# The border between attention gradient and last stage: turning the last dS block on TensorE, and the loads in the order of the program

## The chip, the cores and the metric

The kernel runs on one core of a Trainium2 chip. The core has a matrix engine (TensorE, PE in the profile; its weight loads are PEld), a vector engine (VectorE, DVE), a scalar engine (ScalarE, ACT), a general one (GpSimd, POOL) and a queue that only issues transfers (SyncE, SP). Sixteen DMA engines move data. Each engine runs its own instructions in order and waits for others by semaphores. The metric is the device time of one execution in microseconds; the time before is the median of three executions.

## The reference

One transformer block with adaptive layer norm, its output and the gradients of all its inputs but one bias. There are 2048 tokens of width 512, 32 heads of width 16, and a dense part of width 1792 with a squared ReLU:

```python
h = _layernorm(x) * (1 + ca) + sa
x = x + ga * A(h, wqkv, wo)            # attention
h = _layernorm(x) * (1 + cb) + sb
x = x + gb * B(h, w1, b1, w2, b2)      # dense part
out, vjp = jax.vjp(f, A_x, A_wqkv, A_wo, B_w1, B_b1, B_w2, B_b2, c, w_mod)
grads = vjp(grad_out)
```

All arrays are bf16. What matters here is the end of the backward pass: the gradients dQ, dK and dV of attention, and from them the gradient of the block's input, of `wqkv`, and of the modulation weights.

## The kernel before, in words

The attention gradient goes over eight groups of four heads (`hg`), four chunks of 512 keys (`kc`), four chunks of 512 queries (`qc`) and four tiles of 128 queries in each (`qi`). One (hg, kc, qc, qi) is a unit, four units are a block; there are 512 units and 128 blocks. For a unit, PE makes the scores of four heads (`score`), ACT their exponentials E (`expo`), PE the products dO V (`dp_pair`, two heads at a time into a tile of two PSUM banks), and DVE multiplies both into dS (line 1616). dS is used twice. As it stands it goes into the gradient of K (`k_quad`), while E goes into that of V (`v_quad`); both add into one bank, `accVK`. Turned over it goes into the gradient of Q (`dq_quad`), which sums over a whole block into a bank `dqacc`. `dq_out` scales this sum on ACT into `dqtmp`, and POOL adds it to the sum over key chunks (line 1708).

The turning has two ways. Most units go through a DMA transpose that SP issues (`transpose_unit`): two units at once (1 MB, line 1633) or one (line 1631). The fourth unit of every odd block is turned by PE against an identity matrix (`pe_turn`, eight 128x128 transposes into one bank) and copied to SBUF by ACT (line 1774). For the very last block, number 127, the third unit is turned on PE as well (`last_turn`), and DVE copies the fourth. The units one and two of block 127 still go through a DMA transpose.

The order of the instructions on each engine is written out by hand, in two strings of tokens (`order_t` for a block after an odd one, `order_n` otherwise): s is a score, e an exponential, D a dP pair, q a K or V quad, t and T a turn and its copy, d and Q the dQ matmuls and their output, f a filler matmul that adds nothing. After the last block two passes follow in which only the late tokens still do something.

The last stage (pool `phJbig` and below) has dK, dV and dQ as rows of 128 features by 2048 tokens in twelve tiles `xs["vk", 0..7]` and `xs["dq", 0..3]`. Four of these and half of another are still loaded from DRAM (lines 1792 and 1793); the other 64 rows of `xs["dq", 3]`, which come from the last group of heads, are copied within SBUF by four DMAs that POOL issues (line 1799). The weights `wT_all` (1.5 MB) are loaded at line 1797. Then:

- All twelve tiles are turned on PE into token rows (`dq_tok`, `dvk_tok`), two groups of eight 128x128 transposes for a tile (line 1941), 24 groups in all; DVE copies two out of three groups, ACT the third.
- A row loop over 16 tiles of 128 tokens: `dh1` multiplies the twelve tiles with the weights into `pdh` (line 1881), DVE and ACT do the gradient of the layer norm, `row_sums` adds up two rows on PE, `dx_out` stores the input's gradient. `load_x` fetches the input and an earlier gradient for two tiles at a time, into three buffers.
- Twelve products `dwqkv` for the gradient of `wqkv` (line 1914): four with `dq_tok`, four with the first half of `dvk_tok`, four with its second half. Between them stands the work on the modulation weights.

In this stage PE, ACT and DVE follow the program's order; SP's loads and stores are placed by the framework's scheduler. A tile in SBUF takes the place of tiles of the stage before, and its first writer waits until those are no longer used.

Of the kernel before, what the change touches and what calls it, by code (L numbers as in the profile page):

```python
# [14 lines left out]
AF = mybir.ActivationFunctionType  # L15
# [5 lines left out]
P = 128  # L21
# [13 lines left out]
def kernel(  # L35
# [1512 lines left out]
    with ExitStack() as ph:  # L1548
# [53 lines left out]
        def dp_pair(u, pair):  # L1602
# [14 lines left out]
            if qi == 3 and on_pe(u // 4):  # L1617
                held["dS"] = dS_u
            if u == NU - 2:
                held["last"] = dS_u  # L1620
# [4 lines left out]
        def transpose_unit(u):  # L1625
            hg, kc, qc, qi = units[u]
            if qi == 0:
                dqt[u // 4] = tpool.tile([P, 4, 16, P], BF, name="dsT", tag="dsT")
            if on_pe(u // 4) and qi >= 2:
                if qi == 2 and u < NU - 2:  # L1630
                    SP.dma_start(out=dqt[u // 4][:, qi], in_=bst[u][1].rearrange("p h k -> p (h k)"), transpose=True)
# [18 lines left out]
        def last_turn(half):  # L1650
            pt = psx.tile([P, 8, P], BF, name="ptL", tag=("ps0", "ps1")[half])
            for i in range(8):
                kt = i % 4
                PE.transpose(pt[:, i, :], held["last"][:, 2 * half + i // 4, kt * P:(kt + 1) * P], identb[:])
            ACT.activation(dqt[NU // 4 - 1][:, 2, 8 * half:8 * half + 8, :], pt[:], AF.Identity)
# [26 lines left out]
        def dq_quad(b, kt):  # L1682
            hg, kc, qc, _ = units[4 * b]
            if kt == 0:
                cur["dq"] = psx.tile([P, 512], F32, name="dqacc", tag="px")
# [7 lines left out]
        def dq_out(b):  # L1693
# [5 lines left out]
            if kc == 0:  # L1699
# [29 lines left out]
        with tc.manual_schedule(engines={PE.engine, ACT.engine, DVE.engine, SP.engine, POOL.engine}):  # L1729
# [4 lines left out]
            for b in range(NU // 4 + 3):  # L1734
                toks, bank = order_t if on_pe(b - 1) else order_n
                for tok in toks:
# [26 lines left out]
                    elif c == "f" and 0 < nq < 2 * NU:  # L1763
                        keep_warm()
                    elif c == "t" and 0 <= b - 1 < NU // 4:
                        if b == NU // 4:
                            last_turn(i - 1)
                        pe_turn(b - 1, i - 1)
                    elif c == "T" and 0 <= b - 1 < NU // 4:
                        dst, pt = held.pop(i - 1)  # L1770
                        if b == NU // 4:
                            DVE.tensor_copy(dst, pt[:])
                        else:
                            ACT.activation(dst, pt[:], AF.Identity)  # L1774
# [8 lines left out]
    with ExitStack() as ph:  # L1783
        big = ph.enter_context(tc.tile_pool(name="phJbig", bufs=1))
# [3 lines left out]
        psw = ph.enter_context(tc.tile_pool(name="psJw", bufs=3, space=bass.MemoryType.PSUM))  # L1788
        xs["dq", 1], xs["dq", 2], xs["vk", 4], xs["vk", 5] = (hsets[1][key] for key in ("q", "k", "v", "do"))
# [4 lines left out]
        sums = big.tile([P, 6, D], F32, name="sums_bc")  # L1794
        dmod = big.tile([P, 6, D], BF, name="dmod_bc")
        wT = big.tile([P, 12, D], BF, name="wT_all")
        SP.dma_start(out=wT[:], in_=wT_st.rearrange("j p d -> p j d"))
        for h in range(4):
            POOL.dma_start(out=xs["dq", 3][64 + DH * h:64 + DH * h + DH, :], in_=dq_last[32 * h:32 * h + DH, :])
# [4 lines left out]
        def load_x(g):  # L1804
            x0s[g] = big.tile([P, 2, D], BF, name="x0J", tag="x0J", bufs=3)
            SP.dma_start(out=x0s[g][:], in_=x_dram[:, 2 * g:2 * g + 2, :])
            dx1s[g] = big.tile([P, 2, D], BF, name="dx1J", tag="dx1J", bufs=3)
            SP.dma_start(out=dx1s[g][:], in_=dx1_st[:, 2 * g:2 * g + 2, :])

        load_x(0)  # L1810
        load_x(1)
        wms, wtags = {}, ["wmodJ0", "wmodJ1", "wmodJ2"]

        def wmod_tile():
            wtags.append(wtags.pop(0))
            return big.tile([P, 3 * D], BF, name="wmodJ", tag=wtags[-1], bufs=1)

        wmod_tile()
        wmod_tile()
        dvk_tok = [big.tile([P, 4, TT, P], BF, name=f"dvk_tok{i}") for i in range(2)]  # L1820
        wmod_tile()
# [28 lines left out]
        def c_grad(k, h):  # L1850
            part = slice(3 * D * h, 3 * D * h + 3 * D)
            prod = wk.tile([P, 3 * D], BF, name="cprod", tag="cprod", bufs=1)
# [19 lines left out]
        def norm_tile(t):  # L1872
            xns[t] = wk.tile([P, D], BF, name="xn1b", tag="xn1b", bufs=3)
# [4 lines left out]
        def dh1(t):  # L1878
# [8 lines left out]
            prod1 = wk.tile([P, D], BF, name="prod1", tag="prod1", bufs=3)  # L1887
# [23 lines left out]
        def dwqkv(b, ic):  # L1911
# [4 lines left out]
            if b == 0:  # L1916
                wblk = wk.tile([P, D], BF, name="wqblk", tag="prod1", bufs=3)
                ACT.activation(wblk[:], pw[:], AF.Identity)
                SP.dma_start(out=rows[:, 0:D], in_=wblk[:])
            else:  # L1920
                for i in range(2):
                    srcv = pw.rearrange("p (g v d) -> p g v d", v=2, d=DH)[:, :, 1 - i, :]
                    wblk = wk.tile([P, D], BF, name="wqblk", tag=("prod1", "dxn1")[i], bufs=3)
# [126 lines left out]
```

## Time and profile before

| | |
|---|---|
| median of three executions | 2481.53 us (2478.23, 2481.53, 2486.11) |
| the profiled execution | 2484.38 us |
| its span in the profile | 2482.6 us |
| mean granted PE clock | 0.984 |
| attention gradient ends, last score product (dP) of PE starts | 2365.23 us |
| first row product (`pdh`) starts | 2388.73 us |
| last weight-gradient output issued | 2479.29 us |

Times within the profile count from the start of the span. A line of the timeline gives start and length in microseconds, engine, source line, operation, output and inputs, count, and in brackets how long the engine stood idle before and what ended that. PE lines overlap, since matmuls are pipelined. SPq is SP's queue: its length is the time for which the queue was held by issuing, not that of the transfer.

### The profile page before, as it was taken

How to read it: one execution, taken by the hardware profiler on the slowest of the kernel's cores; microseconds unless marked ns; L12 is line 12 of the kernel's file. 1: busy time of each engine (PE TensorE's matmuls, PEld its weight loads, DVE VectorE, ACT ScalarE, POOL GpSimd, SP SyncE). 2: the span in 40 equal slices, each digit the busy share in tenths (PEclk: the TensorE clock that was granted, in tenths of full speed). 3: DMA queues.
4: the chain of work that ended last, by engine and by line, in shares of the span. 5: the costliest groups of instructions: out<-in, count | busy, mean ns of one | idle time of the engine just before them, and what ended most of it. 6: DMA issues, size and time to landing. Idle time of an engine off the chain costs nothing.

```text
span 2482.6 us, 49937 instructions
## 1 busy us (share of the span) xinstructions
PE 2319.5 (93%) x18967; PEld 782.2 (32%) x19052; DVE 1838.7 (74%) x2379; ACT 2302.5 (93%) x3560; POOL 491.3 (20%) x665
## 2 busy tenths in 40 slices
PE   8899899989998998899999999999999999999999
PEld 3232233223322332442333223332233322333244
DVE  6555354355445554578999999999999999999976
ACT  7999999999999999639999999999999999999954
POOL 3111222332544352101111101101011010110100
PEclk9999999999998999999999999999999999999999
DMA  4467463267647775979999999999999999999994
GB/s 148 128 171 177 143 145 102 80 175 131 90 94 160 151 134 104 246 226 169 205 200 206 199 198 205 201 202 206 203 209 197 210 205 202 200 201 220 200 268 134
DMA packets 1187551, 437.17 MB, mean 176 GB/s; under 512 B 1063915, under 2 KB 1158569, under 8 KB 1186926
## 3 DMA queue, kind: packets, MB, share of 16 engines
q1 hardware_dynamic: 1150334, 388.56, 79.2%
q0 software_dynamic: 20000, 27.35, 6.8%
q10 hardware_dynamic: 16976, 18.07, 2.7%
q8 instruction: 149, 2.44, 0.4%
q14 instruction: 92, 0.75, 0.1%
HBM read 98.30 MB, written 70.80 MB: 68 GB/s over the span
## 4 chain that ended last, share of the span: by engine, by line
ACT 40%; PE 38%; issue 8%; DVE 7%; DMA 4%; ACTq 1%; POOL 0%; SPq 0%; DVEq 0%; another core or an unknown queue 0%; POOLq 0%
ACT E_u L1600 24%; ACT ET L578 12%; PE dqacc L1690 4%; PE psST L576 3%; PE psS_A L1594 3%; DMA dsT<-dS_u 2%; ACT dsT L1774 2%; PE accVK L1663 2%; PE pm L233 2%; PE oacc L592 2%; PE psS_B L1594 2%; PE pdh L1881 2%; PE pm L424 2%; PE pm L500 2%; PE pm L410 2%
## 5 line engine op out<-in xcount | busy, mean ns | idle before, releaser
L1616 DVE TENSOR_TENSOR dS_u<-psD_u,E_u 128x1024 bf16<-128x1024 f32 x1024 | 1185.4, 1218 | 66.5 <-PE psD_u L1614 24.2
L578 ACT ACTIVATE ET<-psST 128x1024 bf16<-128x1024 f32 x1024 | 942.4, 1242 | 16.2 <-PE psST L576 15.7
L1600 ACT ACTIVATE E_u<-psS_A 128x512 bf16<-128x512 f32 x768 | 508.9, 663 | 9.6 <-DMA out_dram<-xlast 7.2
L1600 ACT ACTIVATE E_u<-psS_B 128x512 bf16<-128x512 f32 x768 | 502.1, 654 | 7.6 <-issue 1.9
L1614 PE MATMUL psD_u<-iv,ido 32*128 32x512 bf16 x2048 | 408.8, 387 | 0.4 <-DVE dS_u L1616 0.2
L576 PE MATMUL psST<-qt_sb,kt_sb 32*128 32x512 bf16 x2048 | 315.5, 388 | 45.6 <-ACT ET L578 39.2
L1600 ACT ACTIVATE E_u<-psS_C 128x512 bf16<-128x512 f32 x512 | 333.6, 652 | 2.5 <-PE psS_B L1594 0.9
L1594 PE MATMUL psS_B<-ik,iq 32*128 32x512 bf16 x768 | 294.4, 383 | 9.8 <-ACT E_u L1600 2.4
L1594 PE MATMUL psS_A<-ik,iq 32*128 32x512 bf16 x768 | 293.0, 382 | 11.3 <-DVE dwlast L237 1.0
L1708 POOL TENSOR_TENSOR dQacc<-dQacc,dqtmp 128x512 f32<-128x512 f32 x64 | 81.2, 1269 | 849.0 <-ACT dqtmp L1703 849.0
L1594 PEld LDWEIGHTS <-iq 32*128 32x128 bf16 x2048 | 130.1, 91 | 313.4 <-issue 296.2
L1663 PE MATMUL accVK<-dS_u,qz 128*32 128x512 bf16 x2048 | 213.1, 388 | 0.4 <-DVE dS_u L1616 0.2
L592 PE MATMUL oacc<-ET,vaug 128*32 128x512 bf16 x2048 | 208.5, 397 | 3.9 <-DVE ostage L596 3.9
L1672 PE MATMUL accVK<-E_u,dOs_tok 128*16 128x512 bf16 x2048 | 203.1, 385 | 0.0
L1594 PE MATMUL psS_C<-ik,iq 32*128 32x512 bf16 x512 | 193.7, 378 | 4.3
L576 PEld LDWEIGHTS <-kt_sb 32*128 32x128 bf16 x2048 | 84.9, 91 | 326.5 <-issue 305.5
L1690 PE MATMUL dqacc<-dsT,KS_tok 128*32 128x512 bf16 x2048 | 146.4, 384 | 17.0 <-DMA dsT<-dS_u 3.3
L251 DVE COPY part<-pm 128x512 f32<-128x512 f32 (+2 forms) x106 | 65.2, 615 | 120.4 <-PE pm L233 110.9
L1774 ACT ACTIVATE dsT<-ptT 128x1024 bf16<-128x1024 bf16 x126 | 142.8, 1134 | 6.7 <-PE ptT L1646 6.3
L1614 PEld LDWEIGHTS <-ido 32*128 32x128 bf16 x2048 | 105.4, 91 | 101.2 <-issue 94.8
L1663 PEld LDWEIGHTS <-qz 128*32 128x32 bf16 x2048 | 58.5, 94 | 177.2 <-issue 162.2
L1708 POOL TENSOR_TENSOR dQst<-dQacc,dqtmp 128x512 bf16<-128x512 f32 x32 | 40.6, 1268 | 264.1 <-ACT dqtmp L1703 264.1
(420 smaller groups left out, 2687.3 us busy)
## 6 DMA issues: line engine op xcount, KB each, us to landing
p_st<-part POOLq DMA_DIRECT2D x36, 256.0 KB, 4.6
kt_sb<-qkT_st POOLq DMA_DIRECT2D x124, 64.0 KB, 2.9
wA<-in_B_w_dram SPq DMA_DIRECT2D x28, 256.0 KB
wB<-w1T_st SPq DMA_DIRECT2D x21, 256.0 KB
wA<-w2T_st SPq DMA_DIRECT2D x21, 256.0 KB
wB<-in_B_w_dram SPq DMA_DIRECT2D x21, 256.0 KB
p_st<-part POOLq DMA_DIRECT2D x28, 192.0 KB, 5.2
p_st<-part SPq DMA_DIRECT2D x18, 256.0 KB
```

What stands on the lines that cost most here:

```text
L576: PE.matmul(ps[:, hi, :], kt_sb[r:r + 32, kt * P:(kt + 1) * P], qt_sb[r:r + 32, :], start=True, stop=True, tile_position=(r, 0))
L578: ACT.activation(ET[:, 2 * pair:2 * pair + 2, :], ps[:], AF.Exp, scale=SCALE)
L592: PE.matmul(oacc[32 * hq:32 * hq + 32, :], lhsT, ET[:, hq, :], start=(kt == 0), stop=(kt == TT - 1), tile_position=(0, 32 * hq), skip_grou ...
L1594: PE.matmul(psS[:], st["q"][r:r + 32, qt * P:(qt + 1) * P], st["k"][r:r + 32, kc * 512:kc * 512 + 512], start=True, stop=True, tile_positi ...
L1600: ACT.activation(bst[u][0][:, hq, :], sst.pop((u, hq))[:], AF.Exp, scale=SCALE)
L1614: PE.matmul(psD[:, hi, :], st["do"][r:r + 32, qt * P:(qt + 1) * P], st["v"][r:r + 32, kc * 512:kc * 512 + 512], start=True, stop=True, til ...
L1616: DVE.tensor_tensor(dS_u[:, 2 * pair:2 * pair + 2, :], psD[:], E_u[:, 2 * pair:2 * pair + 2, :], ALU.mult)
L1663: PE.matmul(cur["vk"][32 * hq:32 * hq + 32, :], hst[hg]["qz"][:, qt, hq, :], bst[u][1][:, hq, :], start=(qt == 0), stop=False, tile_positi ...
L1672: PE.matmul(acc[32 * hq:32 * hq + DH, :], dOs_tok[:, qt, (hg * 4 + hq) * DH:(hg * 4 + hq + 1) * DH], E_u[:, hq, :], start=False, stop=(qt ...
L1690: PE.matmul(acc[32 * hq:32 * hq + 32, :], KS_tok[:, kc * 4 + kt, h * DH:h * DH + 32], tT[:, :, hq * 4 + kt, :], start=(kt == 0), stop=(kt ...
L1708: POOL.tensor_tensor(dst2, dst, tmp[:], ALU.add)
L1774: ACT.activation(dst, pt[:], AF.Identity)
```

## The change

It has five parts, all of them at the border between the two stages.

- All four units of block 127 are turned on PE. `last_turn(j)` is now called for j from 0 to 7 (unit j // 2, half j % 2): 0 to 3 at the first t token, 4 to 7 at the second. The targets are the three single banks (`ps0`, `ps1`, `px`; the first again for j = 7) and two tiles of two banks each from the pool of the dP products (j = 3 and 4 in one, 5 and 6 in the other): seven banks. ACT copies j = 0, 1, 4, 7, DVE the others. The DMA transpose of block 127 goes.
- The last dQ block sums in bank `ps1`, and DVE scales it and adds it to the sum over key chunks in one operation straight from PSUM (line 1712 after), in place of ACT and POOL.
- The tiles of the last stage stand in two pools. `phJlow` takes those that are loaded or used in the row loop, `phJbig` the weights and the token rows. So the two sets lie over other tiles of the stage before: the weights' load waits for the last E quad and the last dS, the first load of the input waits for the last dQ matmuls and the last turn copies.
- SP follows the program's order in the last stage too. The four copies of 64 rows are issued by SP, after the first `load_x`; `load_x` in the loop stands at the end of its turn instead of at its start.
- The second half of `dvk_tok` (four tiles) is turned by four DMA transposes, issued in turns 3, 5, 7 and 9 of the row loop, in place of eight of the 24 groups on PE.

```diff
+            if u >= NU - 4:
+                held[qi] = dS_u
+            elif qi == 3 and on_pe(u // 4):
                 held["dS"] = dS_u
-            if u == NU - 2:
-                held["last"] = dS_u
...
+            if u >= NU - 4:
+                return
             if on_pe(u // 4) and qi >= 2:
-                if qi == 2 and u < NU - 2:
+                if qi == 2:
                     SP.dma_start(out=dqt[u // 4][:, qi], in_=bst[u][1].rearrange("p h k -> p (h k)"), transpose=True)
...
-        def last_turn(half):
-            pt = psx.tile([P, 8, P], BF, name="ptL", tag=("ps0", "ps1")[half])
+        def last_turn(j):
+            qi, half = j // 2, j % 2
+            if j in (3, 5):
+                held["pd"] = psd.tile([P, 2, 8, P], BF, name="ptL2", tag="pd")
+            if 3 <= j < 7:
+                pt = held["pd"][:, (j - 3) % 2]
+            else:
+                pt = psx.tile([P, 8, P], BF, name="ptL", tag=("ps0", "ps1", "px")[j % 7])[:]
             for i in range(8):
                 kt = i % 4
-                PE.transpose(pt[:, i, :], held["last"][:, 2 * half + i // 4, kt * P:(kt + 1) * P], identb[:])
-            ACT.activation(dqt[NU // 4 - 1][:, 2, 8 * half:8 * half + 8, :], pt[:], AF.Identity)
+                PE.transpose(pt[:, i, :], held[qi][:, 2 * half + i // 4, kt * P:(kt + 1) * P], identb[:])
+            dst = dqt[NU // 4 - 1][:, qi, 8 * half:8 * half + 8, :]
+            if j in (0, 1, 4, 7):
+                ACT.activation(dst, pt, AF.Identity)
+            else:
+                DVE.tensor_copy(dst, pt)
...
-                cur["dq"] = psx.tile([P, 512], F32, name="dqacc", tag="px")
+                cur["dq"] = psx.tile([P, 512], F32, name="dqacc", tag="ps1" if b == NU // 4 - 1 else "px")
...
-            if kc == 0:
+            if b == NU // 4 - 1:
+                DVE.scalar_tensor_tensor(out=st["dq"][:, qc * 512:(qc + 1) * 512], in0=acc[:], scalar=SCALE, in1=dst,
+                                         op0=ALU.mult, op1=ALU.add)
+            elif kc == 0:
...
+                    elif c == "t" and b == NU // 4:
+                        for j in range(4 * i - 4, 4 * i):
+                            last_turn(j)
...
+        low = ph.enter_context(tc.tile_pool(name="phJlow", bufs=1))
         big = ph.enter_context(tc.tile_pool(name="phJbig", bufs=1))
...
+        ph.enter_context(tc.manual_schedule(engines={PE.engine, ACT.engine, DVE.engine, SP.engine}))
...
+        load_x(0)
         for h in range(4):
-            POOL.dma_start(out=xs["dq", 3][64 + DH * h:64 + DH * h + DH, :], in_=dq_last[32 * h:32 * h + DH, :])
+            SP.dma_start(out=xs["dq", 3][64 + DH * h:64 + DH * h + DH, :], in_=dq_last[32 * h:32 * h + DH, :])
...
-        with tc.manual_schedule(engines={PE.engine, ACT.engine, DVE.engine}):
-            for k, (key, i) in enumerate(order):
+        if True:
+            for k, (key, i) in enumerate(o for o in order if o[0] == "dq" or o[1] < 4):
...
-                if t % 2 == 0 and t >= 2 and t // 2 + 2 < TT // 2:
-                    load_x(t // 2 + 2)
...
+                if t in (3, 5, 7, 9):
+                    i = 4 + (t - 3) // 2
+                    SP.dma_start(out=dvk_tok[1][:, i - 4], in_=xs["vk", i][:], transpose=True)
...
+                if t % 2 == 0 and t >= 2 and t // 2 + 2 < TT // 2:
+                    load_x(t // 2 + 2)
```

Left out are the lines in which `sums`, `dmod`, the `wmod` tiles, `cprod`, `xn1b`, `prod1` and the tiles of `load_x` change their pool, and where tiles are named earlier or later in the program without other effect.

## The prediction

> **What bounds the kernel now.** I read the page first (the span, the engines' shares), then the chain of waits over the last 120 us, then the timeline around the border between the attention gradient and the last stage, then SP's own queue, then the half-microsecond windows there. The page shows a kernel in which PE and ACT are each 93% busy; such a kernel has few gaps, and a change at one border can only be worth what stands still there.
>
> ```profile
> span 2482.6 us, 49937 instructions
> PE 2319.5 (93%) x18967; PEld 782.2 (32%) x19052; DVE 1838.7 (74%) x2379; ACT 2302.5 (93%) x3560; POOL 491.3 (20%) x665
> ```
>
> The chain of waits at the border (start, length, what): the reader is to see two transfers, 8.22 and 12.50 us, between the last score work and the first row product (pdh), with 16 dQ matmuls between them.
>
> ```profile
> 2365.62 0.38 PE ptL L1654 x5
> 2366.00 8.22 DMA dsT<-dS_u
> 2374.27 1.86 PE dqacc L1690 x16
> 2376.18 12.50 DMA wT_all<-wT_st
> 2388.73 0.39 PE pdh L1881
> ```
>
> SP's queue (start, time the queue was held): a transpose of 1 MB holds it for about 5 us, so the last one, though its data was ready, is issued at 2366.00, and every load of the last stage waits behind it.
>
> ```profile
> 2360.93 4.97 SPq L1633 DMA_TRANSPOSE dsT<-dS_u  x1
> 2366.00 4.87 SPq L1633 DMA_TRANSPOSE dsT<-dS_u  x1
> 2370.93 0.58 SPq L1792 DMA_DIRECT2D iq<-dQc  x1
> 2373.53 0.51 SPq L1793 DMA_DIRECT2D qz<-dQc  x1
> 2376.18 0.38 SPq L1797 DMA_DIRECT2D wT_all<-wT_st  x1
> ```
>
> The timeline, with idle time before each and its releaser, shows that PE is nearly as late as the weights: after its 3.31 us of waiting it has turns until 2388.3 and then waits only 0.38 us. So both have to become shorter.
>
> ```profile
> 2374.27 1.84 PE L1690 MATMUL dqacc<-dsT,KS_tok 128*32 128x512 bf16 x16 [3.31 <-DMA dsT<-dS_u]
> 2378.45 2.07 POOL L1799 DMA_DIRECT2D qz<-dQst  x4 [0.30 <-POOL dQst L1708]
> 2387.29 0.61 PE L1941 MATMUL ptq<-identb,qz 128*128 128x128 bf16 x8 [1.05 <-DVE dvk_tok L1947]
> 2388.73 0.39 PE L1881 MATMUL pdh<-wT_all,iq 128*128 128x512 bf16 x1 [0.38 <-DMA wT_all<-wT_st]
> DMA to landing us min/median/max: 7.0/7.1/7.3
> ```
>
> The last of these lines belongs to the four copies of line 1799: 2380.0 + 7.1 is 2387.1, just before 2387.29. The DVE copy named there ended at 2385.8, so the 1.05 us were a wait for those copies. The windows (PE, PEld, DVE, ACT, POOL busy; granted clock; DMA share; GB/s) show the clock at half after the idle stretch and two transfer rates.
>
> ```profile
> 2373.50:2374.00 0.50, 0.00 (x0) 0.00 (x0) 0.00 (x0) 0.00 (x0) 0.00 (x0) 1.00 1.02 369
> 2375.00:2375.50 0.50, 0.50 (x12) 0.17 (x4) 0.00 (x0) 0.00 (x0) 0.00 (x0) 0.50 1.37 377
> 2380.00:2380.50 0.50, 0.50 (x13) 0.50 (x11) 0.45 (x2) 0.47 (x1) 0.50 (x2) 1.00 1.06 156
> 2383.00:2383.50 0.50, 0.50 (x13) 0.50 (x10) 0.45 (x2) 0.50 (x1) 0.00 (x0) 1.00 1.10 352
> 2385.00:2385.50 0.50, 0.50 (x13) 0.50 (x11) 0.50 (x2) 0.18 (x2) 0.00 (x0) 1.00 0.95 158
> ```
>
> **The change, part by part.** Nothing before the last block changes, so times to 2365.55 stand. From there I set the new order against the old rows.
>
> *Turns of the last block.* Four groups of eight PE transposes become eight (0.49 us from group to group, 2365.55 to 2366.04); one DMA transpose goes. Groups 0 to 3 run to 2367.4, the E quad and two filler matmuls to 2368.1. Group 4 shares a two-bank tile with group 3 and waits for DVE's copy of it: last dS ends 2367.1, two copies at 0.69 (row L1772; 0.61 back to back) end 2368.4. Group 6 waits likewise for the copy of group 5: 2370.3. Group 7 ends 2371.2. ACT's four copies at 1.02 (row L1655) end 2372.5 and hold up nobody. Fillers and the last two quads take 0.86 (2368.33 to 2369.19 before), to 2372.05; two dQ blocks at 0.95 each then end at 2373.9 instead of 2376.1. Gain here 2.2; the 3.3 us wait and the half clock behind it (1.7 us lost: 3.4 us at half) go.
>
> *Last dQ by VectorE.* ACT 0.60 and POOL 1.27 are replaced by one DVE operation. No row has its shape: 0.42 (L1904, bf16 difference) and 1.22 (L1616, twice the elements from PSUM) bound it; L1906, the same operation, took 0.75, and I take 0.7. It delays DVE's first turn copy by that much, which the four banks there hide; without them it would cost 0.7.
>
> *Fewer turns in the last stage.* 24 groups become 16: PE loses 8 x 0.445 = 3.6, DVE five copies, ACT three. From 2373.95, the first 14 groups end at 2380.2. In their place SP issues four transposes of 512 KB inside the row loop, about 2.2 us of queue each (row L1631: 2.02 to 2.31) while the DMA share is 0.66, then 0.21 (2400 to 2440); they are wanted at about 2464. I cost them at nothing; the cover is that slack, and its loss is a rival below.
>
> *Weights.* Their tile now lies where the E and dS buffers were, so the load waits for the last E quad, 2372.05, not for dQ and the last copies: issue 2372.4 instead of 2376.18. The four big loads ahead of it issue at 2366.0 instead of 2370.93.
>
> *The four row copies* (the 64 rows of the last dQ) move from POOL's queue to SP's, behind weights, x0 and dx1. This is where the gain is spent. Data of the last transpose stopped at 2372.9 and landed 2374.27: 1.4 us. In order, before: 2.1 MB at 376 GB/s to 2378.6; the 64-row load and POOL's copies, narrow, some 0.5 MB at 160 to 180, and 1.57 MB of weights at 352 (4.45 us) give about 2387.1, landed 2388.5; measured 2388.73, so the order holds. After: data from 2368.1; four loads to 2373.8; 64 rows (1.8) to 2375.6; weights to 2380.1, landed 2381.5; x0 and dx1 (0.52 MB, 1.5) to 2381.6; four copies (issued by 2378.2) 1.3 to 2.4, landed 2384.7. The 7.1 us of before, from 2378.2, would say 2385.3. Bounds: all at 376 GB/s, 2382.0; the weights' own 12.5 us again, then 1.5 and 2.4, 2388.8. I take 2384.7, next to both middle values.
>
> The Trainium skill ("DMA: Bandwidth & Descriptors", Queues, rings and completion order) says that each DMA engine takes a queue's descriptors in ring order. By that rule a copy put behind the weights can't pass them; the landing worked out above agrees.
>
> PE then stands from 2380.2 to 2384.7, and needs two more groups, 0.9, before pdh. Clock: 3.3 us of idling was followed by 3.4 us at 0.50, and 1.05 us (2386.2) by none; 4.5 lies beyond the first, so I take the same 1.7 us (bounds 0 and 3.4, twice as long at half).
>
> The Trainium skill ("TensorE: Matmul & The Clock Gate", Part 1) says that a wholly idle free-running window of some 3.4 us throttles. By that rule 4.5 us of idling need not contain one; then the sum would be 1.7 us better.
>
> **Sum.** Pdh starts in effect at 2384.7 + 0.9 + 1.7 = 2387.3, 1.4 us earlier than 2388.73. The row loop (PE 19.95 of 20 us) and the weight products after it keep their length. The profiled execution took 2484.38 around its span of 2482.6, 2.85 over the median of 2481.53; less 1.4 it is 2483.0, or 2480.1 at the median. I say 2480.
>
> **Rivals.**
> *Copies in time.* If the narrow copies do not wait for x0 and dx1, or the DMA runs at its best rate, PE is the bound: 2373.95 + 16 x 0.445 + 0.15 = 2381.2, 7.5 us gained, 2474.0. For it: 16 groups are all that PE has; against it: 352 GB/s on the weights and the order found above.
> *The row loop starves (slower).* SP in program order puts each x0 load behind an output store that waits for DVE's dx, and behind a transpose. Load of pair 3 issues about 11.7 us after pdh starts and is wanted at 20.3. It decides when landing takes over 8.6 us: were it 12.5 as for the weights, 3.9 are lost at first and about 1.4 at each of four later pairs, 9.5 in all: 2480.1 + 9.5 = 2489.6. Against it: the DMA share there.
> *Copies at the late end.* Landed 2388.8, pdh in effect at 2391.4: 2.7 lost, 2484.2. The change then does not do what it says: one wait takes the place of another.
>
> **How the numbers follow.** Forecast 0.55, copies in time 0.24, late end 0.12, starving 0.09. About 0.3% (7.4 us) is what a measurement of this kernel can tell: faster means below 2474.1, which holds the greater part of "in time", 0.17; slower is starving, 0.09; the rest, 0.74, is no change that can be told. The range 2473.0 to 2485.5 takes in the bounds of the copies and leaves out starving and a little of "in time". The forecast's own: 2477 to 2482.5.
>
> **What would show it.** The last dQ matmuls end near 2373.9 with no DMA named ahead of them; the weights issue near 2372.4 and land by 2382; PE's longest wait in the border stands before the transposes of qz, 3 to 5 us, released by a DMA of the row copies, with the clock at half after it. Wrong if that wait is missing, if pdh waits for the weights instead, or if PE has gaps in the row loop ended by DMA or ACT.

## The result: slower by 0.35%, and the profile after

Nineteen executions of the changed kernel have a median of 2488.34 us (2482.91 to 2499.88), nineteen of the kernel before, run beside them, 2480.71 us (2475.03 to 2489.85). The ratio is 1.0035, with a 95% interval of 1.0023 to 1.0047. The forecast was 2480.0 us in a range of 2473.0 to 2485.5, so it was wrong. Nearest came the rival of the starving row loop, priced at 2489.6 with a chance of 0.09. A second series of the two kernels, run 6 below, has a smaller difference (ratio 1.0014).

The profiled execution of the changed kernel took 2487.6 us. Its page shows nothing of the loss, since 8 us are 0.3% of the span:

```profile
span 2485.8 us, 49959 instructions
PE 2323.8 (93%) x19020; PEld 781.9 (31%) x19020; DVE 1835.2 (74%) x2377; ACT 2300.6 (93%) x3558; POOL 487.0 (20%) x660
```

In this trace the border went as forecast. In the timeline after (start, length, engine, line, what; in brackets the idle time before and its releaser) SP has the four big loads under way at 2364.38 in place of 2370.93, the weights at 2371.53 in place of 2376.18, and then the four row copies. Below stand the last dS, by which I line up the kernels (it ends at 2364.51 + 1.21 = 2365.72, and at 2367.12 before, so 1.40 us of each difference in time stem from what lies ahead), PE's wait for the copies and the first row product.

```profile
2364.38 0.57 SPq L1807 DMA_DIRECT2D iq<-dQc  x1
2364.51 1.21 DVE L1616 TENSOR_TENSOR dS_u<-psD_u,E_u 128x1024 bf16<-128x1024 f32 x1
...
2371.53 0.88 SPq L1813 DMA_DIRECT2D wT_all<-wT_st  x1
...
2374.42 2.47 SPq L1826 DMA_DIRECT2D qz<-dQst  x4
...
2383.36 1.63 PEld L1953 LDWEIGHTS <-qz 128*128 128x128 bf16 x16 [4.48 <-DMA qz<-dQst]
...
2385.05 0.63 PE L1893 MATMUL pdh<-wT_all,iq 128*128 128x512 bf16 x1
```

The windows after (PE, PEld, DVE, ACT, POOL busy; granted clock; DMA share; GB/s) show what that wait costs: the clock is at 0.50 behind it, and the share of the DMA engines is 1.09 while PE stands.

```profile
2379.72:2381.72 2.00, 0.00 (x0) 0.00 (x0) 0.00 (x0) 0.39 (x1) 0.00 (x0) 1.00 1.09 223
2381.72:2383.72 2.00, 0.33 (x4) 0.36 (x5) 0.00 (x0) 0.00 (x0) 0.00 (x0) 0.88 1.09 288
2383.72:2385.72 2.00, 2.00 (x17) 1.63 (x15) 1.12 (x2) 0.00 (x0) 0.00 (x0) 0.50 1.05 391
```

Then the row loop, from the first `pdh` to the first weight product (`pwq`), takes 53.32 us in place of 47.92. The chain of waits says why. Before, it ran through PE's row products (shares by line, from 2389 to 2436 us):

```profile
by line: PE pdh L1881 87.2%; PE rsumJ L1900 13.2%; issue 0.6%
```

After, it alternates between a store that has to land, a transpose that holds SP's queue, and at the end a load of the input:

```profile
2397.13 2.27 DMA out_dram<-dx1J
2399.42 0.33 SPq L1822
...
2399.80 3.02 SPq L1973
...
2402.87 0.57 SPq L1838
...
2403.55 3.80 DMA out_dram<-dx1J
...
2407.80 3.07 SPq L1973
...
2411.60 3.92 DMA out_dram<-dx1J
...
2416.39 3.56 SPq L1973
...
2420.67 4.72 DMA out_dram<-dx1J
...
2430.54 5.77 DMA x0J<-in_A_x_dram
...
2436.39 0.82 ACT xn1b L1886
```

From one store to the next SP needs 2411.60 - 2403.55 = 8.05 us: the store lands (3.86 to the issue of the `dx1` load, which takes over the stored buffer), that load's issue (0.34), the transpose (3.07), the modulation weights (0.57), and gaps. PE needs 6.04 us for the same two tiles. So the input's loads are issued 6.4, 8.0, 9.1 and 9.4 us after one another (2397.62, 2404.04, 2412.08, 2421.16, 2430.54), and the loop falls behind them. ACT's waits in the loop (total, times, longest) and the place where PE at last stands:

```profile
ACT xn1b L1886 <- DMA x0J<-in_A_x_dram: 13.6, 3, 7.3
...
PE rsumJ L1912 <- DVE s12a L1900: 4.0, 1, 4.0
```

PE hides most of ACT's first two waits (1.24 and 5.09 us), since its row products need no `xn1b`; the third (7.30), behind its last product, costs it 4.0 us, and the first weight product behind that runs at half clock again (from `pwq` to the end 47.43 us, 45.95 before).

### The profile page after: what moved, and what is told of

Read it like the earlier page. It is cut to its first block, busy times and chain, and to the rows that moved or that the text cites. A ratio compares the mean times of both kernels' runs of the same rounds, so it can differ in the third digit from the quotient of the medians.

```text
span 2485.8 us, 49959 instructions
## 1 busy us (share of the span) xinstructions
PE 2323.8 (93%) x19020; PEld 781.9 (31%) x19020; DVE 1835.2 (74%) x2377; ACT 2300.6 (93%) x3558; POOL 487.0 (20%) x660
## 4 chain that ended last, share of the span: by engine, by line
ACT 42%; PE 36%; issue 8%; DVE 7%; DMA 3%; SPq 1%; ACTq 1%; POOL 0%; DVEq 0%; POOLq 0%
ACT E_u L1600 25%; ACT ET L578 13%; PE dqacc L1702 4%; PE psST L576 3%; PE psS_A L1594 3%; PE pm L233 2%; ACT dsT L1787 2%; PE accVK L1675 2%; PE oacc L592 2%; PE psS_B L1594 2%; PE pm L500 2%; PE pm L424 2%; PE pm L410 2%; PE pwq L1926 2%; PE psS_C L1594 2%
## 5 line engine op out<-in xcount | busy, mean ns | idle before, releaser
L592 PEld LDWEIGHTS <-vaug 128*32 128x32 bf16 x2048 | 53.1, 93 | 122.6 <-issue 122.6
```

The source lines that it names most:

```text
L592: PE.matmul(oacc[32 * hq:32 * hq + 32, :], lhsT, ET[:, hq, :], start=(kt == 0), stop=(kt == TT - 1), tile_position=(0, 32 * hq), skip_grou ...
```

## The experiments

All kernels are the changed one with the edit shown, unless it says otherwise. Whole times scatter, mostly by 10 to 20 us within one kernel, and most of this is made ahead of the border: in the traces the last dS ends anywhere from 2355.19 to 2372.61, in kernels that differ only behind it. So each trace is read from there on, in three pieces: last dS to the first `pdh`, the row loop, and `pwq` to the end. The last column but one is what the half clock takes from the loop: the sum of (1 - granted clock) over its first microseconds, in windows of 1 us. The last is what is left of the loop over 47.92 us, PE's own time. Pieces that reach to the end of the span are good to 0.05 us, since the span is given in tenths. Each row is one trace.

| kernel | dS to pdh | loop | pwq to end | dS to end | half clock | starved |
|---|---|---|---|---|---|---|
| before | 21.61 | 47.92 | 45.95 | 115.48 | 0 | 0 |
| before, second trace | 20.40 | 47.93 | 45.98 | 114.31 | 0 | 0 |
| after | 19.33 | 53.32 | 47.43 | 120.08 | 0.80 | 4.6 |
| after, second trace | 20.95 | 54.81 | 47.69 | 123.45 | 2.14 | 4.8 |
| all groups on TensorE | 20.44 | 48.91 | 45.75 | 115.10 | 1.00 | 0.0 |
| SP placed by the framework | 19.78 | 48.50 | 46.01 | 114.29 | 0.58 | 0.0 |
| four buffers for dx1 | 19.88 | 49.75 | 45.96 | 115.59 | 1.85 | 0.0 |
| transposes late | 18.96 | 49.34 | 45.99 | 114.29 | 1.44 | 0.0 |
| transposes on ACT's queue | 19.62 | 51.14 | 46.02 | 116.78 | 1.97 | 1.3 |
| late, x0 early, copies first | 16.80 | 47.91 | 45.97 | 110.68 | 0 | 0.0 |
| the same, second trace | 19.32 | 48.92 | 46.00 | 114.24 | 1.01 | 0.0 |
| late, x0 early, copies by POOL | 19.28 | 48.75 | 45.78 | 113.81 | 0.83 | 0.0 |
| late, x0 early, copies by ACT | 18.78 | 49.60 | 46.03 | 114.41 | 1.71 | 0.0 |
| last block alone | 18.93 | 47.92 | 45.96 | 112.81 | 0 | 0 |

Three theories stood against each other. A: SP's queue works in series, a store's landing and a transpose's hold add up past PE's 6.04 us. B: the transposes' own traffic makes the loads late, whatever the order. C: the store's landing alone, in program order, is enough.

**All groups on TensorE again (1).**

```diff
-                if t in (3, 5, 7, 9):
-                    i = 4 + (t - 3) // 2
-                    SP.dma_start(out=dvk_tok[1][:, i - 4], in_=xs["vk", i][:], transpose=True)
-            for k, (key, i) in enumerate(o for o in order if o[0] == "dq" or o[1] < 4):
+            for k, (key, i) in enumerate(order):
```

> All 24 groups are turned on PE again, no DMA transposes in the row loop; SP's program order with each x0 load behind a store, and everything at the border, stay. Theory A (SP's queue in series: a store has to land, then 3.0 to 3.6 us of a transpose hold the queue, then the next store): a period without the transpose is about 2.3 + 0.4 + 0.6 + 0.5 us of SP's own per pair, under PE's 6.04, so the row loop (first pdh to first pwq, 48.1 us before, 53.3 after the change) comes back to 48.1 to 48.6. The eight groups more stand in PE's wait for the row copies (4.48 us), so pdh starts at 19.6 us after the first turn of the last block (20.4 after the change, 23.2 before) at full clock; time 3.6 us under before, 2477. Theory B (the transposes' own load on the DMA engines makes the loads late): the same. Theory C (the store's landing alone, in series on SP, starves the loop): the loop stays at 52 to 53 us, time 2481 to 2483.

Measured: 2477.37 us, ratio to before 0.9981 (0.9960 to 1.0001); no wait of ACT for `x0`, nothing starved. C falls: the program's order and the store's landing are still there. The chain of the row loop is PE's again, and SP's queue in the timeline stands idle for 3 us ahead of each store:

```profile
by line: PE pdh L1893 81.9%; PE rsumJ L1912 14.1%; PE pwq L1926 4.1%; issue 0.5%
```

```profile
2399.37 0.39 SPq L1921 DMA_DIRECT2D out_dram<-dx1J  x1
2399.85 0.42 SPq L1820 DMA_DIRECT2D x0J<-in_A_x_dram  x1
2401.64 0.33 SPq L1822 DMA_DIRECT2D dx1J<-dx_st  x1
2402.02 0.42 SPq L1838 DMA_DIRECT2D wmodJ<-in_w_mod_dram  x1
2405.41 0.39 SPq L1921 DMA_DIRECT2D out_dram<-dx1J  x1
```

It also shows a part of B: from a store's issue to the `dx1` load that waits for it there are 2.19, 2.27, 2.19, 3.06 and 4.10 us here, and 2.29, 3.86, 3.93, 4.74 and 5.65 with the transposes. From the second store on, each landing is some 1.6 us longer with a transpose ahead, besides the 3.0 to 3.6 us on the queue. The border fell short of the expectation: PE still waited 1.98 us for the copies, and the clock fell to 0.50 behind it, so `pdh` starts 22.0 us after the first turn of the last block (20.44 after the last dS), where 19.6 were expected.

**SP placed by the framework (2).**

```diff
-        ph.enter_context(tc.manual_schedule(engines={PE.engine, ACT.engine, DVE.engine, SP.engine}))
+        ph.enter_context(tc.manual_schedule(engines={PE.engine, ACT.engine, DVE.engine}))
```

> As after the change, but SP's instructions in the last stage are placed by the framework again; the four transposes stay. In the program as built, the x0 load of pair 3 now stands ahead of the first store and the first transpose; pairs 4 to 7 each one to two transposes earlier than with the program's order. Theory A: the loads come in time, the row loop is 48.1 plus 0.9 for the half clock at its start, 49.0; time 2479 (pdh 2.75 us earlier than before, 0.9 lost again). Theory B: transposes of the same number and size load the DMA engines as much, x0 lands 4 to 6 us after issue as after the change, and the loop stays at 52 to 53; time 2485 to 2488.

Measured: loop 48.50 us, of it 0.58 by the clock, nothing starved; 2486.34 us, ratio 0.9999 (0.9981 to 1.0018). B alone falls: all four transposes are in the loop, two of them hold the queue even longer, and the DMA share is 0.95 to 1.06 from 2398 to 2422, but each load from the second on stands two stores further ahead than in the changed kernel. It does not stand further ahead of the transposes, as the expectation has it: the second load comes behind two of them, and behind one in the changed kernel. So the stores' place is what differs. The timeline of this kernel:

```profile
2395.04 0.38 SPq L1820 DMA_DIRECT2D x0J<-in_A_x_dram  x1
2395.46 3.30 SPq L1973 DMA_TRANSPOSE dvk_tok<-iv  x1
...
2399.43 3.14 SPq L1973 DMA_TRANSPOSE dvk_tok<-ido  x1
2402.68 0.52 SPq L1820 DMA_DIRECT2D x0J<-in_A_x_dram  x1
...
2404.28 0.39 SPq L1921 DMA_DIRECT2D out_dram<-dx1J  x1
2404.71 5.21 SPq L1973 DMA_TRANSPOSE dvk_tok<-vkb  x1
```

The expected time, 2479, missed by 7 us; the trace's 114.29 from the last dS on is 1.2 us under before, where some 2 were expected, and its last dS ended at 2372.61, the latest of all.

**Four buffers for dx1 (3).** This takes the store's landing out of the series and leaves the transposes.

```diff
-            dx1s[g] = low.tile([P, 2, D], BF, name="dx1J", tag="dx1J", bufs=3)
+            dx1s[g] = low.tile([P, 2, D], BF, name="dx1J", tag="dx1J", bufs=4)
```

> As after the change, with four buffers for dx1 in place of three, so that SP's dx1 load no longer waits for the store issued just ahead of it, but for the store of the pair before. Transposes and order stay. Theory A: SP's period per pair falls from 8 to 9.4 us to 3.5 to 5, below PE's 6.04; the loop is 49.0 us (48.1 plus 0.9 of half clock) up to 50, time 2479 to 2480. Theory B: x0 loads still land 4 to 6 us after issue behind transposes, and are issued only some 5.5 us before ACT wants them: the loop stays at 51 to 53, time 2483 to 2488.

Measured: loop 49.75 us, of it 1.85 by the clock; 2485.11 us, ratio 1.0000 (0.9981 to 1.0019). The loads are issued 6.4, 6.1, 7.6 and 7.2 us apart; ACT still waits for two of them, 5.5 us together, but PE never does. One link less in the series is enough. The loop lies in theory A's range; the whole time lies in B's, but at a ratio of 1.0000 it tells nothing of the loop.

**Transposes behind the last load (4).**

```diff
-                if t in (3, 5, 7, 9):
-                    i = 4 + (t - 3) // 2
+                if t in (11, 12, 13, 14):
+                    i = 4 + t - 11
```

> As after the change, with the four transposes issued in turns 11 to 14, behind the last x0 load, in place of turns 3, 5, 7 and 9. Theories A and B both: x0 loads have neither transposes ahead of them on SP nor beside them on the DMA engines; loop 49.0 us, time 2479, unless the last output stores and the weight products are now late (the second half of dvk_tok is wanted some 25 us after the loop: not expected). Theory C (the store's landing alone): loop 52 to 53, time 2484 to 2488.

Measured: loop 49.34 us, of it 1.44 by the clock; 2481.71 us, ratio 0.9988 (0.9974 to 1.0001). Loads are issued 6.4, 5.7, 6.0 and 6.0 us apart, and the stores land in 2.26, 2.30, 2.21, 2.96 and 4.04 us, as without transposes. The products that use the second half of `dvk_tok` show no wait.

**Transposes on ACT's queue (5).**

```diff
-                    SP.dma_start(out=dvk_tok[1][:, i - 4], in_=xs["vk", i][:], transpose=True)
+                    ACT.dma_start(out=dvk_tok[1][:, i - 4], in_=xs["vk", i][:], transpose=True)
```

> As after the change, but the four transposes of the row loop are issued by ACT's queue in the same turns 3, 5, 7 and 9, not by SP's. The transfers, their size and their time stay; only the 3.0 to 3.6 us for which each holds a queue leave SP. ACT is busy 1.6 of 3.0 us in a turn there, so a hold makes it late by some 1.6 us, which the two PSUM banks of pdh cover. Theory A (SP's queue in series): SP issues an x0 load every 6.04 us, the row loop is 48.5 to 49.5 us (53.3 after the change), and from the end of the last dS to the end of the span it is 114.5 us (120.1 after the change, 115.5 before). Theory B (the transposes' load on the DMA engines): x0 lands as late as after the change and the loop stays at 51 to 53.

Measured: loop 51.14 us, inside B's range and outside A's; 2479.95 us, ratio 0.9996 (0.9981 to 1.0012). Read with the clock it says something between: 1.97 us are half clock, 1.3 us are starved, against 4.6 to 4.8. So without the hold on SP's queue some three quarters of the loss are gone. What remains has two possible parents. The stores land in 4.5 to 8.0 us, more than the 6.04 us that PE takes, and ACT itself stands behind its transposes, up to 4.7 us, so that DVE and with it the stores are late. Its timeline:

```profile
2409.85 4.71 ACTq L1973 DMA_TRANSPOSE dvk_tok<-ido  x1
2414.67 0.81 ACT L1886 ACTIVATE xn1b<-x0J,nb,rstd 128x512 bf16<-128x512 bf16 x1 [4.03 <-issue]
...
2433.79 0.81 ACT L1886 ACTIVATE xn1b<-x0J,nb,rstd 128x512 bf16<-128x512 bf16 x1 [4.96 <-DMA x0J<-in_A_x_dram]
```

I had costed ACT's hold at 1.6 us behind two PSUM banks; that was too little, and it spoils this run as a clean test. How the remaining quarter divides between traffic and ACT was not tried further.

**The changed kernel again (6).** No edit.

> The changed kernel itself once more, beside the others. Theory A: the same chain again, x0 loads of pairs 4 to 7 issued 8.0 to 9.4 us after one another, row loop 52 to 55 us, last dS to end 119 to 122; time 5 to 8 us over before. Rival: the first trace caught a chance delay; then the loop is 48 to 50 and time within 2 us of before.

Measured: 2484.45 us, ratio 1.0014 (0.9995 to 1.0034). This is 2.1 us over the median before in its series (2482.40), not the expected 5 to 8, and the interval takes in 1: by whole times this series alone can't tell the kernels apart. The trace shows the chain again: loads 7.0, 7.9, 9.1 and 9.3 us apart, 4.8 us starved. From the last dS to the end the two traces of each kernel have a mean of 121.8 after and 114.9 before: 6.9 us, near the 7.6 us between the first medians.

**Late transposes, x0 early, row copies first (7, 8).**

```diff
-                if t in (3, 5, 7, 9):
-                    i = 4 + (t - 3) // 2
+                if t in (11, 12, 13, 14):
+                    i = 4 + t - 11
...
+        for h in range(4):
+            SP.dma_start(out=xs["dq", 3][64 + DH * h:64 + DH * h + DH, :], in_=dq_last[32 * h:32 * h + DH, :])
         load_x(0)
-        for h in range(4):
-            SP.dma_start(out=xs["dq", 3][64 + DH * h:64 + DH * h + DH, :], in_=dq_last[32 * h:32 * h + DH, :])
...
             SP.dma_start(out=x0s[g][:], in_=x_dram[:, 2 * g:2 * g + 2, :])
+            if g < 3:
+                load_dx1(g)
+
+        def load_dx1(g):
             dx1s[g] = low.tile([P, 2, D], BF, name="dx1J", tag="dx1J", bufs=3)
...
             for t in range(TT):
+                if t % 2 == 0 and t >= 2 and t // 2 + 2 < TT // 2:
+                    load_x(t // 2 + 2)
...
                     dx_out(t - 1)
                 if t % 2 == 0 and t >= 2 and t // 2 + 2 < TT // 2:
-                    load_x(t // 2 + 2)
+                    load_dx1(t // 2 + 2)
```

> The transposes in turns 11 to 14, the x0 half of each load at the start of its turn (the dx1 half at the end, behind the store), and the four row copies ahead of the first x0 and dx1 loads on SP, not behind them. If the copies wait in SP's ring for what stands ahead of them, they land 1.5 us sooner (0.52 MB at 352 GB/s less ahead): PE's wait for them falls from 4.5 to 3.0 us, pdh starts 17.5 to 17.9 us after the last dS (19.0 to 19.9 in the runs with the copies behind; 21.6 before), and the loop, which has 0.9 us less at half clock, is 48.1 to 48.6. Last dS to end 112.5 to 113, time 2.5 to 3 us under before. If they don't wait for those loads, pdh stays at 19 to 19.9.

> The kernel with late transposes, early x0 and the row copies ahead of x0 once more, for its time beside the others and a second trace. Theory: pdh 16.8 us after the last dS, loop 47.9, last dS to end 110 to 111.5 (115.5 before, 120 to 123.5 after the change), so 4 to 5 us (0.2%) faster than before and 9 to 12 faster than the changed kernel, if the stages ahead are left as they are. Rival: the first trace of it was a lucky one; then pdh 18 or later and time equal to before.

Measured: 2481.72 us, ratio 0.9998 (0.9980 to 1.0016), and again 2480.54 us, ratio 0.9989 (0.9973 to 1.0004). In the first trace PE waited 2.58 us for the copies at full clock, and `pdh` came at 16.80, better than expected; in the second it waited 4.45, the clock fell, and `pdh` came at 19.32. So of the second run's two expectations the rival came (`pdh` at 18 or later, time equal to before). The same program, with every SP issue up to the copies at the same distance from the last dS (weights +5.81, copies +8.2 in both), differs by 1.9 us in when the copies land (15.91 and 17.78, where PE's waits end); the half clock adds the rest. The weights were late already: SP's second `dx1` load waits for them to land, and it is issued 14.11 us after the last dS in the first trace and 16.25 in the second. Its lines there:

```profile
2378.13 0.33 SPq L1826 DMA_DIRECT2D dx1J<-dx_st  x1
```

```profile
2383.21 0.33 SPq L1826 DMA_DIRECT2D dx1J<-dx_st  x1
```

PE's wait for the copies ends 1.80 and 1.53 us behind that. In the seven traces in which the copies stand behind x0 and dx1 on SP (the changed kernel twice, and runs 1 to 5) it ends 3.86 to 4.55 us behind it. So the place ahead of x0 is worth some 2 us and more. What scatters is the weights' landing: 13.45 to 16.25 us after the last dS in the ten traces where this load dates it, all with the same issue at 5.8; the second trace's is the latest.

**The copies on other queues (9, 10).** The last kernel, with POOL or ACT in place of SP for the four copies.

```diff
-            SP.dma_start(out=xs["dq", 3][64 + DH * h:64 + DH * h + DH, :], in_=dq_last[32 * h:32 * h + DH, :])
+            POOL.dma_start(out=xs["dq", 3][64 + DH * h:64 + DH * h + DH, :], in_=dq_last[32 * h:32 * h + DH, :])
```

> As the kernel with the copies ahead of x0, but POOL issues the four copies, as before the change. If what delays them after the change is the place in SP's ring behind the 1.5 MB of weights, they now go beside the weights: issued 1.8 us after the last dQ sum starts, landed some 7.1 us later as before the change, that is at about 15.4 us after the last dS; weights then some 1 us later than 13.7 us after the last dS; pdh at 16.2 to 17 us, no wait over 1.5 us and no half clock, loop 47.9 to 48.2; last dS to end 110 to 111.5, time 4 to 5.5 us under before. If the DMA engines' rate for the sum of all bytes is what counts, pdh comes at 17.5 to 19 as with SP.

> As the kernel with late transposes, early x0 and the copies first, with the four row copies issued by ACT's queue in place of SP's. If the place in SP's ring behind the 1.5 MB of weights is what the copies wait for, they land some 3 to 4 us after their issue, at 11 to 12.5 us after the last dS, PE waits for them under 0.5 us, and pdh starts at 15.0 to 15.8, where the 16 groups end; loop 47.9, last dS to end 109.3 to 110. If the DMA engines' rate for all the bytes decides, they land no sooner than with SP: pdh 16.5 to 19, end 110.5 to 113.

Measured: POOL 2483.36 us, ratio 1.0005 (0.9992 to 1.0018), `pdh` at 19.28; ACT 2481.20 us, ratio 1.0000 (0.9984 to 1.0015), `pdh` at 18.78. Both miss what was expected of a queue of their own by 2.3 us and more, and lie where SP's copies lie (16.8 to 19.3). In these two runs another queue does not carry the copies past the weights' 1.5 MB. The DMA queues of ACT's run show when its copies moved. In the 4.40 us behind their first issue (2378.80 to 2383.20) only SP's queue, q1, moved packets (packets, MB, share of 16 engines); in the next 4.40 us ACT's queue, q10, moved the copies' 0.26 MB beside it:

```profile
q1 hardware_dynamic: 1459, 1.48, 109.2%
```

```profile
q1 hardware_dynamic: 650, 0.76, 86.6%
q10 hardware_dynamic: 128, 0.26, 23.5%
```

That the rate of the engines for all bytes holds them back is argued from this, not shown. It is also no rule that they stay behind: in the kernel before, POOL's copies were issued 2.27 us after the weights and landed ahead of them (PE's wait for the copies ended at 2387.29, that for the weights at 2388.73).

**The kernel before again (11), and the last block alone (12).** The first has no edit; the second is the kernel before with the change's diff up to and with the loop over tokens, and the last stage as it was.

> The kernel before once more, for a second trace of it. If one trace speaks for the kernel, pdh starts 21.0 to 22.2 us after the last dS (21.6), the row loop takes 47.9 to 48.3 us and from the last dS to the end it is 115 to 116.2 us (115.5). If it was a chance, these move by as much as between the two traces of the changed kernel (loop 53.3 and 54.8, end 120.1 and 123.5).

> The kernel before with the first two parts of the change alone: the last dS block turned on TensorE over seven banks, the last dQ summed by VectorE. The last stage is that of before: one pool, POOL issues the row copies, 24 groups on TensorE, SP placed by the framework. If these two parts carry the border's gain, the last dQ ends 7.0 us after the last dS as with the change (9.0 before), PE has turns until 7.0 + 24 x 0.445 = 17.7, POOL's copies land at 10.0 + 7.1 = 17.1, pdh starts at 17.8 to 18.6 (21.6 before), no wait over 1.5 us; loop 47.9 to 48.3; last dS to end 111.7 to 113, time 2.5 to 3.8 us under before, 8 to 10 under the changed kernel. If the two pools and the order of loads are what brings it, pdh stays at 20.5 to 21.6.

Measured: before, one execution of 2482.73 us, loop and weight products as in the first trace to 0.03 us, but `pdh` 1.2 us sooner, which misses the expected 21.0 to 22.2. There PE waited 2.58 us for the copies, and its last transpose landed sooner (last dQ at 7.3 us after the last dS, 9.0 in the first trace). The last block alone: 2478.77 us, ratio 0.9986 (0.9973 to 0.9999), the only version whose interval lies below 1, by little; the changed kernel had 1.0035 and 1.0014. Its last dQ ends 7.0 us after the last dS, as with the whole change. Its timeline at the border, with POOL's copies and 24 groups:

```profile
2363.67 2.07 POOL L1812 DMA_DIRECT2D qz<-dQst  x4 [0.30 <-POOL dQst L1723]
...
2373.23 0.61 PE L1954 MATMUL ptq<-identb,qz 128*128 128x128 bf16 x8 [1.14 <-DMA qz<-dQst]
...
2374.12 0.38 PE L1894 MATMUL pdh<-wT_all,iq 128*128 128x512 bf16 x1
```

`pdh` starts 18.93 us after the last dS, a little over the expected 17.8 to 18.6. The wait is 1.14 us and `pdh` runs at full speed from its first matmul (0.38; 0.63 after the change). In its one trace these two parts alone bring the border all that the whole change brings, and more. Why more is not shown: run 1, too, has 24 groups for PE to do while the copies are under way, and its `pdh` comes at 20.44.

## Why the prediction was wrong

**Right in the first trace: what the border gives.** Set against the last dS, the last dQ was forecast to end at 6.8 us and ended at 7.0; the copies to land at 17.6, and PE's wait for them ended at 17.6; PE's wait 4.5 us, measured 4.48; `pdh` "in effect" at 20.2, measured 19.33 + 0.80 of half clock = 20.1. So the 1.4 us of gain against the first trace of before came as summed. The clock's term was right too: two groups before `pdh` took 1.7 us in place of 0.9, and the loop lost 0.80, together 1.6 where I took 1.7. The case in which the sum would have been 1.7 better did not come: PE stood still for a whole interval of the clock's beat (2379.82 to 2383.23, see the last section). The other traces show how much of this was luck. `pdh` in effect came at 23.1 in the second trace after, with 2.9 us lost to the clock, and at 20.4 in the second one before. Over the six traces that have this border unaltered (the changed kernel twice, and runs 2 to 5) its mean is 21.2, against 21.0 for the two traces before: no gain that these traces can tell. The landing of the weights moves by 2.8 us from trace to trace (runs 7, 8), which is more than the gain. And one sum does not come out: 2378.6, some 0.5 MB at 160 to 180 GB/s and 4.45 us give 2385.9 to 2386.3 and not 2387.1, so the order of the transfers was confirmed less closely than it says.

**Wrong: "I cost them at nothing; the cover is that slack".** This is the step that failed, and with it "The row loop ... and the weight products after it keep their length". The four transposes are wanted late, and their results were never late. But the cover that mattered was not theirs. It was that of what stands behind them on SP: the next store, and behind that the next load. The sum had the hold (2.2 us, from row L1631; here 3.0 to 3.6, and up to 5.2 in the run with SP placed by the framework), but did not add it to the store's landing in one series. Added, with rows that were there, it would have been: a landing of 2.15 to 4.96 us (from a store to the `dx1` load that waits for it), 2.2, and three issues of about 0.5: 5.9 to 8.7 us against PE's 6.04. The longest and the shortest landing in SP's queue before:

```profile
2400.03 0.39 SPq L1909 DMA_DIRECT2D out_dram<-dx1J  x1
...
2404.99 0.32 SPq L1808 DMA_DIRECT2D dx1J<-dx_st  x1
...
2418.16 0.38 SPq L1909 DMA_DIRECT2D out_dram<-dx1J  x1
2420.31 0.33 SPq L1808 DMA_DIRECT2D dx1J<-dx_st  x1
```

That is a loop at its limit or past it, where I had seen one with slack. Measured, the series took 8.0 to 9.4 us from the second turn on. A share of 0.66 and 0.21 of the DMA engines says nothing on a queue that waits.

**The rival was the right place with the wrong switch.** It was priced at 9.5 us and "decides when landing takes over 8.6 us". The loads that ACT waited for landed in 4.1 to 5.8 us, never in 8.6; they were issued late, the gaps between them 0.4, 2.0, 3.0 and 3.3 us over PE's 6.04. Measured, 4.6 to 4.8 us are starved in the loop and 1.5 to 1.7 us lost by the half clock behind it, 6.1 to 6.5 in all. The prediction's own sign of being wrong came with it: a gap of PE in the row loop (4.0 us), at the end of a chain of waits from DVE through ACT to the load. Its chance, 0.09, rested on the landing and was too small for that reason.

**Half right: what the Trainium skill says of a queue's order.** I had cited "DMA: Bandwidth & Descriptors" (Queues, rings and completion order) for copies that can't pass the weights in their ring. That section gives the order in which descriptors are taken, and says itself that a later one may finish first, so "can't pass" went beyond it. In the traces the copies on SP landed behind the weights every time, and sooner by some 2 us when they stood ahead of x0 and dx1: within one queue the place counted. But the copies on POOL's and ACT's queues, which have no weights ahead of them, landed no sooner, so the ring's order is not the whole reason.

**Explained in part:** the 10 to 20 us by which whole executions of one kernel differ. They go with the granted clock. Of 99 executions of the kernel before, the fastest (2471.47 us) has a mean clock of 0.991 and the slowest (2498.37) one of 0.982; 0.009 of the span is 22 us. In the fourteen traces the half clock ahead of the last dS takes 22 to 41 us, and without it the time of the last dS scatters by 2.6 us (standard deviation) in place of 5.0. Why one execution has more of it than another is open.

## What to carry to other kernels

When an instruction is put on a queue "in the slack", look at that queue as at an engine: add up, for one turn of the loop, every hold and every wait that the queue's program order now puts in series, and compare the sum with the turn of the engine that sets the pace; the busy share of the DMA engines does not show it. Where a load reuses the buffer of a store issued just ahead of it, the store's landing is in that sum; one more buffer, or the load ahead of the store, takes it out. And when a change has several parts, measure the one that is nearest to the bound alone: here the first two parts alone were the only version whose interval (0.9973 to 0.9999) lies below 1, and the transposes behind the stores on SP cost the loop 4.6 to 4.8 us.

## What the runs showed of the hardware that was not expected

- A transpose of 512 KB held the queue for 3.0 to 3.6 us in the row loop (up to 5.2 with the DMA share near 1), while the same size took 2.0 to 2.3 in the attention gradient. A 256 KB store issued behind one landed some 1.6 us later than without.
- How long PE may stand before the clock falls is no single number. Waits of 2.58 us were followed by full clock twice, but one of 2.62 us (copies by ACT) and one of 1.98 us (all groups on TensorE) by half clock, as one of 3.31 us was before. The timelines of the run with all groups on TensorE and of the first one with the copies ahead of x0, at the wait (in the first, the line names an `x0` load that landed at the same time as the copies) and at the first row product, which takes 0.63 us at half clock and 0.38 at full:

```profile
2379.48 0.91 PE L1953 MATMUL ptq<-identb,qz 128*128 128x128 bf16 x8 [1.98 <-DMA x0J<-in_A_x_dram]
...
2381.04 0.63 PE L1893 MATMUL pdh<-wT_all,iq 128*128 128x512 bf16 x1
```

```profile
2379.93 0.61 PE L1957 MATMUL ptq<-identb,qz 128*128 128x128 bf16 x8 [2.58 <-DMA qz<-dQst]
...
2380.82 0.38 PE L1897 MATMUL pdh<-wT_all,iq 128*128 128x512 bf16 x1
```

- What decides is where the wait falls. In the trace's record of the granted clock the spells of half clock start a whole number of 3.413 us apart, over the whole span of each of the fourteen traces, and last one, two or three times that. Around the border (2355 to 2400 us) an interval of this beat at full clock was followed by half clock when PE was busy in it for 1.43 us or less, and by full clock when it was busy for 1.74 or more, in all fourteen. The wait of 1.98 us lay within one interval; the first one of 2.58 was divided by a boundary (counted from other spells of that trace). The windows of these two traces by the beat, PE's busy time first and the granted clock third from the end:

```profile
2376.22:2379.63 3.41, 1.43 (x27) 1.29 (x24) 2.11 (x4) 1.14 (x2) 0.00 (x0) 1.00 0.92 233
2379.63:2383.04 3.41, 3.19 (x20) 2.17 (x20) 0.78 (x2) 1.92 (x3) 0.00 (x0) 0.50 1.05 399
```

```profile
2375.54:2378.95 3.41, 1.81 (x33) 1.64 (x30) 2.19 (x4) 2.24 (x3) 0.00 (x0) 1.00 1.11 243
2378.95:2382.36 3.41, 2.43 (x24) 1.64 (x25) 1.37 (x3) 0.33 (x1) 0.00 (x0) 1.00 1.06 357
```

  It is no whole rule: earlier in the span half clock also follows intervals in which the profile shows PE busy throughout.
- Once the half clock is taken out, PE's row loop is the same to 0.03 us in every kernel that doesn't starve (47.92 us): the windows' granted clock, summed as 1 minus itself, accounts for the rest.
